# Decode attention plus FFN on one core: the sum is turned to five rows of 128 by a bf16 matmul, and the store has five runs of 256 B instead of 128 of 10 B

## Chip, cores and metric

The kernel runs on one core of one Trainium2 chip. The metric is device microseconds (us) of an execution, and quoted times are medians of a few runs. The *span* of a profile (first to last instruction) is about 1.6 us shorter than the time of the same run.

## The reference, cut to what matters

A decode step for one token: layer norm of `x` (640 numbers), attention of 32 heads over a cache of 32768 positions each, plus a SwiGLU FFN, plus the residual. The K and V caches are 537 MB and are read once.

```python
xn = _layernorm(x)
return x + _A_ref(xn, k_cache, v_cache, wq, wo) + _B_ref(xn, w_gate, w_up, w_down)
# _A_ref: q = xn @ wq; per head softmax(q k^T / sqrt(128)) v; then (32*128) @ wo -> 640
# _B_ref: (silu(xn @ w_gate) * (xn @ w_up)) @ w_down -> 640
```

## The kernel before

K and V of each head go whole (8.4 MB) through a ring of three slots, asked for by one queue (SP). VectorE (DVE) multiplies K by q, TensorE (PE) adds up the scores and multiplies P by V. After the last head comes the tail, which is all that this study is about. The last V is loaded in five pieces of 128, 64, 32, 16 and 16 column blocks, each with its semaphore.

```python
wd_v = wd.rearrange("p j (m c) -> p j m c", c=NCD)      # NCD = 5
wo_v = wo.rearrange("p h (m c) -> p h m c", c=NCD)
acc = ps8[:, 6, 0:NCD]                                  # PSUM, output m*5+c at [m, c]
...
def pv_last():                                          # PE
    for i, n in enumerate(TAIL):                        # 128, 64, 32, 16, 16
        t.wait_ge(s_tail[i], 16)
        for _ in range(n):
            mm = t.matmul(OL, lhsT=ring[:, s, j * DH:(j + 1) * DH], rhs=P[:, h % PR, j:j + 1], ...)   # L292
def att(h):
    for c in range(NCD):                                # weights 10 B apart
        mm = t.matmul(acc[:, c:c + 1], lhsT=wo_v[:, h, :, c], rhs=ocol[:, h:h + 1], ...)              # L358
...
fold(H - 2)
t.wait_ge(s_wo, 16)
t.wait_ge(s_ov, H)
for h in range(H - 1):
    att(h)                                              # 155 matmuls
total(H - 1)
pv_last()                                               # 256 matmuls
t.wait_ge(s_ov, H + 1)
att(H - 1).then_inc(s_att, 1)                           # 5 matmuls
...
v.wait_ge(s_att, 1)                                     # DVE
v.tensor_tensor(out=outb[:, :], in0=xf[:, :], in1=acc, op=ALU.add).then_inc(s_fin, 1)
...
e.wait_ge(s_fin, 1)                                     # SP: 128 runs of 10 B
e.dma_start(out[0, 0:1, :].rearrange("o (p c) -> (o p) c", c=NCD), outb[:, :]).then_inc(s_out, 16)
```

Of the kernel before, what the change touches and what calls it, by code (L numbers as in the profile page):

```python
# [5 lines left out]
ALU = mybir.AluOpType  # L6
ACTF = mybir.ActivationFunctionType
AX = mybir.AxisListType
BF16 = mybir.dt.bfloat16
F32 = mybir.dt.float32  # L10


def bass_parallel_sum__gqa_block_cached__swiglu_ffn__decode_kernel(
# [18 lines left out]
    NCD = D // 128  # L32
# [41 lines left out]
    with ExitStack() as es:  # L74
        def sbt(name, shape, dtype):
            return es.enter_context(nc.sbuf_tensor(name, shape, dtype))

        def sem(name):
            return es.enter_context(nc.semaphore(name))
# [5 lines left out]
        ident = sbt("ident", [128, 128], BF16)  # L85
# [3 lines left out]
        ocol = sbt("ocol", [128, H], BF16)  # L89
        hcol = sbt("hcol", [128, FB], BF16)  # L90
        sg = sbt("sg", [128, 2, FB], F32)
        one1 = sbt("one1", [1, 1], BF16)
        xf = sbt("xf", [128, NCD], F32)
        xc = sbt("xc", [128, NCD], F32)
        xq = sbt("xq", [128, NCD], F32)
        xn = sbt("xn", [128, NCD], BF16)
        outb = sbt("outb", [128, NCD], BF16)
# [8 lines left out]
        s_x, s_wq, s_wo, s_out = sem("x"), sem("wq"), sem("wo"), sem("o")  # L106
# [10 lines left out]
        s_fpd, s_fx = sem("ffn_down"), sem("ffn_x")  # L117
        s_exp, s_pv, s_o4, s_fold, s_ov = sem("exp"), sem("pv"), sem("o4"), sem("fold"), sem("ov")
        s_f, s_fa, s_fd = sem("ffn_pe"), sem("ffn_act"), sem("ffn_dve")
        s_att, s_fin = sem("att"), sem("fin")  # L120
        block = es.enter_context(nc.Block())

        flat = ring[:, :, :].rearrange("p s n -> p (s n)")
# [2 lines left out]
        xrow = flat[0:1, x0 + NCD * 128:x0 + NCD * 128 + D]  # L126
# [8 lines left out]
        wd = flat[:, d0:d0 + FB * D].rearrange("p (j d) -> p j d", j=FB)  # L135
        assert 2 * NCD * F + FB * D <= CE
        wg_v = wg.rearrange("p (c n) -> p c n", c=NCD)
        wu_v = wu.rearrange("p (c n) -> p c n", c=NCD)
        wd_v = wd.rearrange("p j (m c) -> p j m c", c=NCD)

        def hidden(w, c, j):
            if j < FM:
                return w[:, c, 0:FM * 128].rearrange("p (m j) -> p m j", j=FM)[:, :, j]
            return w[:, c, FM * 128:F]
        wo = flat[:, WO_S * CE:WO_S * CE + H * D].rearrange("p (h n) -> p h n", h=H)
        wo_v = wo.rearrange("p h (m c) -> p h m c", c=NCD)
        assert H * D <= CE

        def kv_src(cache, h, j0, n):
            return cache[0, h].rearrange("(p j) d -> p (j d)", p=128)[:, j0 * DH:(j0 + n) * DH]  # L150
# [20 lines left out]
        with nc.psum_tensor("ps8", [128, 8, 512], F32) as ps8:  # L171
# [3 lines left out]
            acc = ps8[:, 6, 0:NCD]  # L175
            fold_ps = ps8[:, 6, 8:9]
            misc = ps8[:, 7, :]

            @block.sync
            def sp(e):  # L180
                owner = {}
                for u in units:
                    s = slot_of[u]
                    if s in owner:
                        e.wait_ge(*owner.pop(s))
                    if u[0] == "wq":
                        e.dma_start(wq, A_wq.rearrange("(p c) n -> p (c n)", c=NCD)).then_inc(s_wq, 16)
                        owner[s] = (s_q, NQB)
                    elif u[0] == "k":
                        e.dma_start(ring[:, s, :], kv_src(A_k_cache, u[1], 0, NJ)).then_inc(s_slot[s], 16)  # L190
                        owner[s] = (s_qk, NHF * (u[1] + 1))
                    elif u == LASTV:
                        j = 0
                        for i, n in enumerate(TAIL):
                            e.dma_start(ring[:, s, j * DH:(j + n) * DH],
                                        kv_src(A_v_cache, u[1], j, n)).then_inc(s_tail[i], 16)
                            j += n
                    elif u[0] == "v":
                        e.dma_start(ring[:, s, :], kv_src(A_v_cache, u[1], 0, NJ)).then_inc(s_slot[s], 16)
                        owner[s] = (s_pv, u[1] + 1)  # L200
                    elif u[0] == "ffn":
                        e.dma_start(wg, B_w_gate.rearrange("(p c) n -> p (c n)", c=NCD)).then_inc(s_ffn, 16)
                        e.dma_start(wu, B_w_up.rearrange("(p c) n -> p (c n)", c=NCD)).then_inc(s_ffn, 16)
                        e.dma_start(flat[:, d0:d0 + FM * D], B_w_down[0:FM * 128, :].rearrange(  # L204
                            "(p j) n -> p (j n)", j=FM)).then_inc(s_ffn, 16)
                        e.dma_start(wd[0:FL, FM, :], B_w_down[FM * 128:F, :]).then_inc(s_ffn, 16)
                        owner[s] = (s_fpd, 1)
                    else:
                        e.dma_start(wo, A_wo.rearrange("(h d) n -> d h n", d=DH)).then_inc(s_wo, 16)
                e.wait_ge(s_fin, 1)  # L210
                e.dma_start(out[0, 0:1, :].rearrange("o (p c) -> (o p) c", c=NCD), outb[:, :]).then_inc(s_out, 16)
                e.wait_ge(s_out, 16)

            @block.gpsimd
# [8 lines left out]
            def pe(t):  # L223
# [2 lines left out]
                t.wait_ge(s_a, 2)  # L226
                for c in range(NCD):
                    mm = t.matmul(misc[:, 8 + c:9 + c], lhsT=xrow_v[:, :, c], rhs=one1[:, :], start=True, stop=True)
                mm.then_inc(s_pa, 1)

                t.wait_ge(s_a, 4)
# [6 lines left out]
                for b in range(NQB):  # L238
                    for c in range(NCD):
                        mm = t.matmul(bank[b], lhsT=xnb[:, c, :], rhs=wq_v[:, c, b * 512:(b + 1) * 512],  # L240
                                      start=(c == 0), stop=(c == NCD - 1))
# [97 lines left out]
                for off, w in ((0, wg_v), (FB, wu_v)):  # L339
                    for j in range(FB):  # L340
                        n = 128 if j < FM else FL
                        for c in range(NCD):
                            mm = t.matmul(misc[0:n, off + j:off + j + 1], lhsT=hidden(w, c, j),  # L343
                                          rhs=xn[:, c:c + 1], start=(c == 0), stop=(c == NCD - 1))
# [3 lines left out]
                for j in range(FB):  # L348
                    n = 128 if j < FM else FL
                    for c in range(NCD):  # L350
                        mm = t.matmul(acc[:, c:c + 1], lhsT=wd_v[0:n, j, :, c], rhs=hcol[0:n, j:j + 1],
                                      start=first, stop=(j == FB - 1), skip_group_check=True)
                        first = False
                mm.then_inc(s_fpd, 1)

                def att(h):
                    for c in range(NCD):
                        mm = t.matmul(acc[:, c:c + 1], lhsT=wo_v[:, h, :, c], rhs=ocol[:, h:h + 1],  # L358
                                      start=(h == 0 and c == 0), stop=(h == H - 1), skip_group_check=True)
                    return mm  # L360

# [11 lines left out]
                for h in range(H - 1):  # L373
                    att(h)
                total(H - 1)
                pv_last()
                t.wait_ge(s_ov, H + 1)
                att(H - 1).then_inc(s_att, 1)

            @block.scalar  # L380
            def act(a):
# [53 lines left out]
            def dve(v):  # L435
                n_a = [0]

                def step(ins):
                    ins.then_inc(s_a, 1)
                    n_a[0] += 1  # L440
                    v.wait_ge(s_a, n_a[0])
# [2 lines left out]
                step(v.memset(one1[:, :], 1.0))  # L444
                v.wait_ge(s_pa, 1)
                step(v.tensor_copy(out=xf[:, :], in_=misc[:, 8:8 + NCD]))
                step(v.tensor_reduce(out=st[:, 0:1], in_=xf[:, :], axis=AX.X, op=ALU.add))
                v.wait_ge(s_pa, 2)
                step(v.tensor_scalar(out=st[:, 1:2], in0=misc[:, 0:1], scalar1=1.0 / D, scalar2=None,
# [18 lines left out]
                n = 0  # L468
# [14 lines left out]
                    v.wait_ge(s_fd, n)  # L483

                v.wait_ge(s_fpd, 1)
                v.tensor_tensor(out=xf[:, :], in0=xf[:, :], in1=acc, op=ALU.add).then_inc(s_fx, 1)

                group, wait = counter(v, H0)

# [45 lines left out]
                h = H - 1  # L535
# [2 lines left out]
                v.tensor_scalar(out=ocol[:, h:h + 1], in0=OL, scalar1=rzb[:, h % SR:h % SR + 1],  # L538
                                scalar2=None, op0=ALU.mult).then_inc(s_ov, 1)
                v.wait_ge(s_att, 1)  # L540
                v.tensor_tensor(out=outb[:, :], in0=xf[:, :], in1=acc, op=ALU.add).then_inc(s_fin, 1)


# [26 lines left out]
```

## Time and profile before

| | before |
|---|---|
| median of 3 runs (range) | 1294.11 us (1293.77 to 1294.47) |
| span of the profiled run | 1292.1 us |
| read from HBM | 554 MB at 429 GB/s over the span |
| store: issue to full semaphore | 2.82 us |

The first view is the page of the kernel before. The rows are 40 equal slices of the span: busy tenths of the DMA engines, and what they moved.

```profile
span 1292.1 us, 9830 instructions
...
DMA  9999999999999999999999999999999999999997
GB/s 400 449 424 427 443 425 435 436 434 428 436 434 438 428 436 438 426 434 438 426 434 438 430 432 436 434 432 432 438 434 428 436 438 426 434 438 428 432 401 315
...
q1 hardware_dynamic: 14704, 554.00, 99.5%
q8 instruction: 9, 0.15, 0.0%
```

The DMA engines are the limit in all slices but the last. So a change that does not touch the loads can act only in the tail, some 20 us.

The second view is the end of the chain that ended last in the kernel before: start, length, what.

```profile
1277.65 0.43 PE ps L310 x2
1278.07 1.63 PE ps L292 x61
1279.70 0.23 issue
1279.93 3.55 PE ps L292 x128
1283.48 2.38 issue
1285.86 1.94 PE ps L292 x67
...
1287.82 0.23 DVE ocol L538
...
1288.10 0.37 PE ps L358 x5
...
1288.50 0.16 DVE outb L541
```

"issue" is time in which the engine waited for nothing that the profile knows of. There are two such gaps among the matmuls on the last V (L292), exactly 128 matmuls apart. The third view is the timeline around this stretch: the 155 projection matmuls ahead of it, and the sum and the store issue at its end.

```profile
1271.32 6.33 PE L358 MATMUL ps<-ocol,ring 128*128 128x1 bf16 x155 [0.36 <-ACT ocol L408]
...
1288.50 0.16 DVE L541 TENSOR_TENSOR outb<-xf,ps 128x5 bf16<-128x5 f32 x1 [0.45 <-PE ps L358]
1288.69 0.35 SPq L211 DMA_DIRECT2D out_dram<-outb  x1
```

The last view is what the queue's own engine waited for at the end (total, times, longest, in us).

```profile
SPq L74 <- DMA out_dram<-outb: 2.5, 1, 2.5
```

So a store of 1280 B holds the kernel for 0.35 us of issue and 2.5 us of waiting.

### The profile page before, as it was taken

The page shows a single profiled execution, that of the slowest core. Times are in us where ns is not written, and L with a number is a line of the kernel's source. Part 1 is how long each engine was busy: PE and PEld are TensorE (multiplying, and loading weights), DVE is VectorE, ACT ScalarE, POOL GpSimd, SP SyncE. Part 2 cuts the span into 40 slices and gives each one's busy share as a digit, 9 for nine tenths or more (in the row PEclk, how much of TensorE's full clock was granted, in tenths as well). Part 3 has the DMA queues.
Part 4 walks back from the last instruction along what each step waited for, and adds up shares of the span by engine and source line. Part 5 has one row for each costly group of instructions (what it writes and reads, how often), then busy time and mean ns, then how long its engine had stood idle before and what let it go on. Part 6 is the DMA issues. An engine that isn't in the chain of part 4 may idle for free.

```text
span 1292.1 us, 9830 instructions
## 1 busy us (share of the span) xinstructions
PE 1036.7 (80%) x5147; PEld 263.8 (20%) x3227; DVE 669.9 (52%) x407; ACT 51.9 (4%) x139; POOL 1.1 (0%) x8
## 2 busy tenths in 40 slices
PE   3678879877779877778877778877778877778977
PEld 1301222111222111222111222111222111222115
DVE  0485444666444666444666444666444666444560
ACT  2000000000000000000000000000000000000000
POOL 0000000000000000000000000000000000000000
PEclk9588899888889888899888899888889888889886
DMA  9999999999999999999999999999999999999997
GB/s 400 449 424 427 443 425 435 436 434 428 436 434 438 428 436 438 426 434 438 426 434 438 430 432 436 434 432 432 438 434 428 436 438 426 434 438 428 432 401 315
DMA packets 14717, 554.16 MB, mean 429 GB/s; under 512 B 1329, under 2 KB 5490, under 8 KB 5746
## 3 DMA queue, kind: packets, MB, share of 16 engines
q1 hardware_dynamic: 14704, 554.00, 99.5%
q8 instruction: 9, 0.15, 0.0%
q14 instruction: 2, 0.02, 0.0%
q10 hardware_dynamic: 2, 0.00, 0.0%
HBM read 553.99 MB, written 0.00 MB: 429 GB/s over the span
## 4 chain that ended last, share of the span: by engine, by line
DMA 52%; PE 29%; DVE 12%; issue 6%; SPq 0%; DVEq 0%; ACT 0%
DMA ring<-in_A_k_cache_dram 52%; PE ps L279 17%; DVE ring L504 12%; PE ps L248 9%; PE ps L267 1%; PE ps L292 1%; PE ps L358 1%; PE ps L316 0%; PE ps L310 0%; PE ps L302 0%; DVEq L504 0%; SPq L204 0%; DVE sc L510 0%; PE ps L322 0%; ACT o L403 0%
## 5 line engine op out<-in xcount | busy, mean ns | idle before, releaser
L504 DVE TENSOR_TENSOR ring<-ring,qb 128x8192 bf16<-128x8192 bf16 x128 | 557.8, 4420 | 86.6 <-DMA ring<-in_A_k_cache_dram 86.5
L248 PE MATMUL ps<-ring,ident 128*128 128x512 bf16 x1920 | 496.0, 417 | 0.0
L279 PE MATMUL ps<-ring,P 128*4 128x512 bf16 x1984 | 438.3, 379 | 0.0
L267 PE MATMUL ps<-ring,ident 128*128 128x512 bf16 x128 | 56.1, 438 | 224.2 <-DVE ring L504 223.7
L279 PEld LDWEIGHTS ps<-ring,P 128*4 128x4 bf16 x1984 | 166.0, 85 | 245.4
L267 PEld LDWEIGHTS ps<-ring,ident 128*128 128x128 bf16 x128 | 12.6, 98 | 620.4 <-DVE ring L504 326.4
L522 DVE TENSOR_SCALAR negb<-ps 128x1 f32<-128x1 f32 x32 | 5.1, 158 | 215.5 <-PE ps L322 215.5
L510 DVE TENSOR_REDUCE sc<-ps 128x64 f32<-128x512 f32 x128 | 82.3, 684 | 62.6 <-PE ps L248 62.6
L519 DVE TENSOR_REDUCE m<-ps 1x1 f32<-1x128 f32 x32 | 8.9, 279 | 192.2 <-PE ps L316 192.2
L412 ACT ACTIVATE P<-sc,negb 128x256 bf16<-128x256 f32 x32 | 16.2, 508 | 1179.6 <-DVE negb L522 1179.6
L302 PE MATMUL ps<-identf,o 4*128 4x1 f32 x248 | 31.9, 245 | 0.9 <-ACT o L403 0.9
L310 PEld LDWEIGHTS ps<-rsum,ones 128*128 128x128 f32 x64 | 12.3, 194 | 99.0 <-issue 98.2
L302 PEld LDWEIGHTS ps<-identf,o 4*128 4x128 f32 x248 | 30.0, 187 | 0.9 <-ACT o L403 0.9
L403 ACT ACTIVATE o<-ps,rzb 4x512 f32<-4x512 f32 x31 | 21.0, 677 | 0.0
L240 PE MATMUL ps<-ring 128*128 128x512 bf16 x40 | 10.2, 420 | 11.2 <-DMA ring<-in_A_wq_dram 11.2
L473 DVE TENSOR_SCALAR sg<-sg 128x13 f32<-128x13 f32 (+1 forms) x2 | 0.2, 156 | 34.3 <-ACT sg L393 34.3
L516 DVE TENSOR_REDUCE pmax<-sc 128x1 f32<-128x256 f32 x32 | 13.4, 420 | 0.0
L343 PE MATMUL ps<-xn,ring 128*128 128x1 bf16 (+1 forms) x140 | 8.7, 198 | 5.7 <-DMA ring<-in_B_w_down_dram 5.7
L316 PE MATMUL ps<-identf,pmax 128*1 128x128 f32 x64 | 12.2, 272 | 1.2 <-DVE pmax L516 1.2
L322 PE MATMUL ps<-m,ones 1*128 1x1 f32 x64 | 12.1, 256 | 0.4 <-DVE m L519 0.4
L322 PEld LDWEIGHTS ps<-m,ones 1*128 1x128 f32 x64 | 9.4, 182 | 14.2 <-issue 13.5
L492 DVE RECIPROCAL rzb<-ps 128x1 f32<-128x1 f32 x32 | 5.0, 158 | 9.8 <-PE ps L310 9.8
(50 smaller groups left out, 88.2 us busy)
## 6 DMA issues: line engine op xcount, KB each, us to landing
ring<-in_A_wq_dram SPq DMA_DIRECT2D x1, 5120.0 KB, 15.3
ring<-in_A_wo_dram SPq DMA_DIRECT2D x1, 5120.0 KB, 37.0
ring<-in_A_v_cache_dram SPq DMA_DIRECT2D x1, 4096.0 KB, 22.2
ring<-in_B_w_gate_dram SPq DMA_DIRECT2D x1, 2160.0 KB, 19.9
ring<-in_B_w_up_dram SPq DMA_DIRECT2D x1, 2160.0 KB, 24.6
ring<-in_B_w_down_dram SPq DMA_DIRECT2D x1, 2080.0 KB, 28.6
ring<-in_A_v_cache_dram SPq DMA_DIRECT2D x1, 2048.0 KB, 21.6
ring<-in_A_v_cache_dram SPq DMA_DIRECT2D x1, 1024.0 KB, 23.6
```

Of the source, the lines that this page charges most:

```text
L248: return t.add_instruction(mybir.InstMatmult(start_tensor_calc=False, stop_tensor_calc=stop, tile_size=(128, 128), tile_position=(0, 0), l ...
L267: t.matmul(ob, lhsT=ident[:, :], rhs=src, start=True, stop=False)
L279: mm = t.matmul(O, lhsT=P[:, h % PR, j:j + W], rhs=ring[:, s, j * DH:(j + W) * DH], start=(j == 0), stop=(j + W == NJ))
L292: mm = t.matmul(OL, lhsT=ring[:, s, j * DH:(j + 1) * DH], rhs=P[:, h % PR, j:j + 1], start=(j == 0), stop=(j == NJ - 1))
L302: mm = t.matmul(fold_ps, lhsT=o4[:, m * DH:(m + 1) * DH], rhs=identf[0:W, m:m + 1], start=(m == 0), stop=(m == W - 1))
L322: t.matmul(misc[:, 128:129], lhsT=ones[0:1, :], rhs=m1[0:1, h % SR:h % SR + 1], start=True, stop=True).then_inc(s_b, 1)
L358: mm = t.matmul(acc[:, c:c + 1], lhsT=wo_v[:, h, :, c], rhs=ocol[:, h:h + 1], start=(h == 0 and c == 0), stop=(h == H - 1), skip_group_che ...
L403: a.activation(out=o4[:, :], in_=O, func=ACTF.Copy, scale=rzb[0:W, h % SR:h % SR + 1]).then_inc(s_o4, 1)
L412: a.activation(out=P[:, h % PR, :], in_=sc[:, :], func=ACTF.Exp, bias=negb[:, h % SR:h % SR + 1], scale=c_scale, accum_out=rsum[:, h % SR: ...
L504: v.tensor_tensor(out=kh, in0=kh, in1=q[:, None, :].to_broadcast([128, HF, DH]), op=ALU.mult).then_inc(s_mul, 1)
L510: v.tensor_reduce(out=sc[:, i * HF:(i + 1) * HF], in_=bank[i].rearrange("p (j e) -> p j e", e=G), axis=AX.X, op=ALU.add).then_inc(s_red, 1)
L516: v.tensor_reduce(out=pmax[:, h % SR:h % SR + 1], in_=sc[:, :], axis=AX.X, op=ALU.max).then_inc(s_max, 1)
```

## The change

Its intent is a shorter store. The output is kept as [m, c] with output number `c*128+m`, so that five rows of 128 are whole runs of 256 B. One bf16 matmul with the identity turns the 128x5 sum to 5x128, DVE copies it out of PSUM, and the store has five runs. A second copy of x in that order (`xr`) is made at the start. The order of the columns also changes how the weights of `wo` and `w_down` are read: side by side instead of 10 B apart.

```diff
-        wd_v = wd.rearrange("p j (m c) -> p j m c", c=NCD)
+        wd_v = wd.rearrange("p j (c m) -> p j c m", c=NCD)
-        wo_v = wo.rearrange("p h (m c) -> p h m c", c=NCD)
+        wo_v = wo.rearrange("p h (c m) -> p h c m", c=NCD)
+            orow_ps = ps8[0:NCD, 5, 128:256]
...
-                e.wait_ge(s_fin, 1)
-                e.dma_start(out[0, 0:1, :].rearrange("o (p c) -> (o p) c", c=NCD), outb[:, :]).then_inc(s_out, 16)
+                e.wait_ge(s_fin, 2)
+                e.dma_start(out[0, 0:1, :].rearrange("o (c m) -> (o c) m", c=NCD), orow[:, :]).then_inc(s_out, 16)
...
+                for c in range(NCD):
+                    mm = t.matmul(misc[:, 16 + c:17 + c], lhsT=xrow[:, c * 128:(c + 1) * 128], rhs=one1[:, :],
+                                  start=True, stop=True)
...
-                        mm = t.matmul(acc[:, c:c + 1], lhsT=wo_v[:, h, :, c], rhs=ocol[:, h:h + 1],
+                        mm = t.matmul(acc[:, c:c + 1], lhsT=wo_v[:, h, c, :], rhs=ocol[:, h:h + 1],
...
                 att(H - 1).then_inc(s_att, 1)
+                t.wait_ge(s_fin, 1)
+                t.matmul(orow_ps, lhsT=outb[:, :], rhs=ident[:, :], start=True, stop=True).then_inc(s_or, 1)
...
-                v.tensor_tensor(out=outb[:, :], in0=xf[:, :], in1=acc, op=ALU.add).then_inc(s_fin, 1)
+                v.tensor_tensor(out=outb[:, :], in0=xr[:, :], in1=acc, op=ALU.add).then_inc(s_fin, 1)
+                v.wait_ge(s_or, 1)
+                v.tensor_copy(out=orow[:, :], in_=orow_ps).then_inc(s_fin, 1)
```

(The same edit on `wd_v`'s matmul, the semaphores, the buffers and the copy to `xr` are cut.)

More of the change, by code (lines that the diff above doesn't have):

```diff
@@ L93, in bass_parallel_sum__gqa_block_cached__swiglu_ffn__decode_kernel @@
         xf = sbt("xf", [128, NCD], F32)
+        xr = sbt("xr", [128, NCD], F32)
+        orow = sbt("orow", [NCD, 128], BF16)
         xc = sbt("xc", [128, NCD], F32)
@@ L120, in bass_parallel_sum__gqa_block_cached__swiglu_ffn__decode_kernel @@
         s_att, s_fin = sem("att"), sem("fin")
+        s_xr, s_or = sem("xr"), sem("orow")
         block = es.enter_context(nc.Block())
@@ L350, in pe @@
                     for c in range(NCD):
-                        mm = t.matmul(acc[:, c:c + 1], lhsT=wd_v[0:n, j, :, c], rhs=hcol[0:n, j:j + 1],
+                        mm = t.matmul(acc[:, c:c + 1], lhsT=wd_v[0:n, j, c, :], rhs=hcol[0:n, j:j + 1],
                                       start=first, stop=(j == FB - 1), skip_group_check=True)
@@ L446, in dve @@
                 step(v.tensor_copy(out=xf[:, :], in_=misc[:, 8:8 + NCD]))
+                v.tensor_copy(out=xr[:, :], in_=misc[:, 16:16 + NCD]).then_inc(s_xr, 1)
                 step(v.tensor_reduce(out=st[:, 0:1], in_=xf[:, :], axis=AX.X, op=ALU.add))
@@ L485, in dve @@
                 v.wait_ge(s_fpd, 1)
-                v.tensor_tensor(out=xf[:, :], in0=xf[:, :], in1=acc, op=ALU.add).then_inc(s_fx, 1)
+                v.wait_ge(s_xr, 1)
+                v.tensor_tensor(out=xr[:, :], in0=xr[:, :], in1=acc, op=ALU.add).then_inc(s_fx, 1)
                 group, wait = counter(v, H0)
```

## The prediction

> **What bounds the kernel now.** The page says DMA: 554 MB at 429 GB/s, DMA row 9 in all slices but the last. The median is 1294.11 us, the span 1292.1. All but a tail of some 20 us is reading K and V, which the change does not touch. So only the tail can move the time.
>
> **The tail before** (timeline of the last 40 us, chain of waits):
> - 1271.32 to 1277.65: 155 output-projection matmuls (L358), 41 ns apart.
> - 1277.9 to 1287.8: 256 matmuls on the last V (L292), 27.5 ns apart while they run, with two idle gaps called "issue": 0.23 us at 1279.7 and 2.38 us at 1283.48, exactly 128 matmuls apart.
> - By the trace's semaphore updates the last five V pieces landed at 1275.9, 1280.8, 1283.3, 1284.5 and 1285.7. The matmul that ended the long gap waits for no semaphore, and 16 KB packets on the instruction queue start at 1277.4, 1283.5 and 1287.0. So I read the gap as instruction fetch, not data. The Trainium skill ("Runtime: NRT & Kernel Launch", Instruction fetch mechanics) says that instructions come in 16 KiB blocks of 256; 128 weight loads and 128 matmuls are that number, which agrees.
> - 1287.82 ocol, 1288.10 five matmuls, 1288.50 sum (163 ns), 1288.69 store issue (348 ns); the semaphore is full at 1291.51; end 1292.1.
>
> **What the change does.**
> 1. *Adds* in the last chain: a hop to PE (0.04 us, as from ocol to L358), one matmul (198 ns for the first L358, plus 127 more columns at the granted clock 0.5, about 106 ns), a hop, and a copy of 5x128 (158 ns for one column at L522, plus about 130 ns for 128, estimated from the 128x256 reduce of 420 ns). Together +0.65 us (0.5 to 0.8), fully on the path.
> 2. *Removes* most of the store's spread. From issue end to last landing it takes 2.47 us: first packet after 0.49 us, 144 packets within 0.2 us, then the 16 engines' semaphore updates from 1289.94 to 1291.51. The first engine is back 0.41 us after the first packet, the last 1.8 us. I take that spread as writes of 10 B into shared lines of HBM. Five whole 256 B runs should behave like the first engine: -1.3 us (estimate, -0.2 to -1.6). [...]
> 3. *Unstated in the title:* `wo` and `w_down` weights are now read with columns side by side instead of 10 B apart. L358 should go from 41 ns to L292's 27.5, so the 155 end 2.1 us earlier; L351 saves 1.1 us at 42 us, hidden under the DMA. The 2.1 us let PE reach each instruction block sooner, so the fetch is asked for sooner; the floor is the last V piece (1285.74 + 16 matmuls + drain, 1286.4 against 1287.8). Estimate -0.7 us (0 to -1.4).
> 4. Five more matmuls and a copy at 2.1 us: hidden, as the weights of L240 land at 16.1.
>
> **Sum:** 0.65 - 1.3 - 0.7 = -1.35 us: 1292.8 us, 1291.6 to 1294.2. Far inside 2%.
>
> **What would show it.** L358 mean spacing near 27 ns; the long L292 gap shorter or earlier; between sum and store issue +0.65 us; store issue to landing near 1.3 us instead of 2.8; everything before 1270 us unmoved.
>
> **What would make it wrong.** A fixed write receipt (then about 1294); block boundaries falling worse, with the gap kept; a slow PE wake-up or copy; DMA noise of a few tenths (runs before: 1293.77 to 1294.47).

## The result, and the profile after

After takes 1292.66 us (median of 4, 1291.66 to 1292.86) against 1293.94 us for before in the same rounds. The ratio is 0.9988, with a 95% interval of 0.9971 to 1.0006: the same within 2%, and the interval is not clear of zero, though the runs themselves do not overlap (the slowest of after, 1292.86, lies under the fastest of before, 1293.46). A ratio here is the mean time of one kernel's runs over that of the other's of the same rounds, so it is not quite the ratio of the medians. Executions over 1.5% slower than the fastest of the same kernel are left out of the means. A second measurement (after_again, 5 runs) gave 1292.59 against 1293.84, again without overlap. I had expected 1.2 us below before, and gaps that end near 1279.6 and 1285.8; the time fell by 1.25 us, and the gaps ended at 1280.00 and 1286.21.

The page after:

```profile
span 1291.1 us, 9843 instructions
...
DMA  9999999999999999999999999999999999999998
...
q1 hardware_dynamic: 14570, 554.00, 99.6%
q8 instruction: 9, 0.15, 0.0%
```

The end of the chain after:

```profile
1275.59 0.43 PE ps L317 x2
1276.01 0.07 issue
1276.08 1.63 PE ps L299 x56
1277.71 1.86 issue
1279.58 3.55 PE ps L299 x128
1283.13 2.66 issue
1285.79 2.08 PE ps L299 x72
...
1287.88 0.23 DVE ocol L549
...
1288.16 0.31 PE ps L365 x5
...
1288.49 0.17 DVE outb L552
...
1288.71 0.28 PE ps L387
...
1289.01 0.28 DVE orow L554
```

The timeline of the projection and of the store issue after, and what SP waited for:

```profile
1271.43 4.15 PE L365 MATMUL ps<-ocol,ring 128*128 128x1 bf16 x155 [0.35 <-ACT ocol L417]
...
1289.32 0.36 SPq L215 DMA_DIRECT2D out_dram<-orow  x1
```

```profile
SPq L74 <- DMA out_dram<-orow: 0.8, 1, 0.8
```

| Stage (us) | before | after | change |
|---|---|---|---|
| 155 projection matmuls | 6.33 | 4.15 | -2.18 |
| start of the sum | 1288.50 | 1288.49 | 0.0 |
| start of the sum to store issue | 0.19 | 0.83 | +0.64 |
| store issue to full semaphore | 2.82 | 1.19 | -1.63 |
| span | 1292.1 | 1291.1 | -1.0 |

The last two changes make up the span's change: 0.64 - 1.63 = -0.99. The odd line is the first: PE saved 2.2 us in the projection and then started the sum at the same moment. The gap at 1277.71 grew from 0.23 to 1.86 us. The experiments ask where that went, and why the old store was so slow.

### The profile page after: what moved, and what is told of

It reads as the page before. It is cut to its first block, busy times and chain, and to the rows that moved or that the text cites. A ratio compares the mean times of both kernels' runs of the same rounds, so it can differ in the third digit from the quotient of the medians.

```text
span 1291.1 us, 9843 instructions
## 1 busy us (share of the span) xinstructions
PE 1039.1 (80%) x5152; PEld 261.2 (20%) x3233; DVE 670.2 (52%) x409; ACT 51.9 (4%) x139; POOL 1.1 (0%) x8
## 4 chain that ended last, share of the span: by engine, by line
DMA 52%; PE 31%; DVE 11%; issue 6%; SPq 0%; DVEq 0%; ACT 0%
DMA ring<-in_A_k_cache_dram 52%; PE ps L286 17%; PE ps L255 11%; DVE ring L515 11%; PE ps L274 1%; PE ps L299 1%; PE ps L365 0%; PE ps L323 0%; PE ps L317 0%; PE ps L309 0%; DVEq L515 0%; SPq L208 0%; DVE sc L521 0%; PE ps L329 0%; ACT o L412 0%
## 5 line engine op out<-in xcount | busy, mean ns | idle before, releaser
L299 PE MATMUL ps<-P,ring 128*128 128x1 bf16 x256 | 7.2, 165 | 4.6 <-issue 4.5
```

## The experiments

Two questions. **A: what is the gap in the last-V matmuls?** *Fetch theory*: PE waits for its next 16 KB block of instructions (128 weight loads and 128 matmuls). *Data theory*: it waits for the last V piece, which lands at 1285.74 in before and 1285.96 in after. **B: what made the old store slow?** The number of runs, their size, a fixed receipt, or something that the runs share.

Eleven runs of ten kernels follow, after_again among them. "V landed" is the last semaphore update of the last V piece in the trace's records, and packets are those of the instruction queue (q8), from the same records.

### layout_only (wrong result)

```diff
-wd_v = wd.rearrange("p j (m c) -> p j m c", c=NCD)     # before, weights alone changed; wo_v and the
+wd_v = wd.rearrange("p j (c m) -> p j c m", c=NCD)     # two matmuls likewise
```

> Before with only the wo and w_down reads changed to columns side by side (result wrong on purpose: columns permuted). Fetch theory (the long gap in the last-V matmuls is instruction fetch, asked for when the sequencer dispatches the block ahead, not when the array gets there): the 155 projection matmuls take 4.1 to 4.2 us instead of 6.3, the gap stays and ends within 0.3 us of 1285.86, time within 0.3 us of before. My prediction's theory (the 2.1 us reach the fetch): gap ends 0.7 us or more earlier and the time falls by about 0.7 us. Data theory (the gap waits for the last V piece): gap ends when that piece lands, at 1285.7 to 1286.0, time unchanged.

Measured: 1293.61 us against 1293.86 (5 and 9 runs), ratio 0.9996, interval 0.9983 to 1.001. The timeline:

```profile
1271.96 4.19 PE L358 MATMUL ps<-ocol,ring 128*128 128x1 bf16 x155 [0.35 <-ACT ocol L408]
...
1280.30 3.55 PE L292 MATMUL ps<-P,ring 128*128 128x1 bf16 x128 [1.85 <-issue]
...
1286.23 1.93 PE L292 MATMUL ps<-P,ring 128*128 128x1 bf16 x67 [2.37 <-issue]
```

The projection fell to 4.19 us, and the first gap grew to 1.85 us: the same exchange as in after, with no turn and no new store. The gap's end, 1286.23, misses the 0.3 us that I had allowed (0.37 off), but this run's tail is late as a whole: its V landed at 1286.40, 0.66 us after before's. The gap ended 0.17 us before V landed, so it did not wait for the last piece, and the pieces that the next 35 matmuls need had landed by 1283.93. The interval, -2.2 to +1.3 us, holds zero and the predicted -0.7 us alike, so the times alone do not decide. The trace says more: the last-V matmuls ended 1.76 us after V landed, against 2.05 us in before, so at most some 0.3 us was gained here and not 0.7. The clock is no rival for the faster projection: the clock of before fell from 1.0 to 0.5 at 1271.7 us and that of after at 1273.3 us, but the matmuls of before are 40 ns apart on both sides of the fall, and those of after 25 and then 27 ns.

### store_only (wrong result)

```diff
-e.dma_start(out[0, 0:1, :].rearrange("o (p c) -> (o p) c", c=NCD), outb[:, :])
+e.dma_start(out[0, 0:1, :].rearrange("o (c m) -> (o c) m", c=NCD), orow[:, :])   # orow: zeros, set at the start
```

> Before, but the store is five runs of 256 B from a tile of zeros made at the start (result wrong on purpose). If the store's gain and the turn's cost simply add: issue to landing 1.2 us instead of 2.8, sum to issue unchanged at 0.19 us, time 1.6 us below before. If the gain in after came from elsewhere (the tail before the store): within 0.5 us of before.

Measured: 1292.23 us against 1293.86, so -1.63 us; ratio 0.9988 (0.9974 to 1.0001). The semaphore is full 1.18 us after issue, and the sum stays 0.19 us ahead of it. SP waited for it as in after:

```profile
SPq L74 <- DMA out_dram<-orow: 0.8, 1, 0.8
```

The interval just reaches 1, but no run of store_only (1292.16 to 1292.40) comes near one of before (1293.44 to 1294.52). The size of the store's part, 1.63 us, is the same in the time and in the trace.

### turn_only (wrong result)

```diff
-e.dma_start(out[0, 0:1, :].rearrange("o (c m) -> (o c) m", c=NCD), orow[:, :])   # after
+e.dma_start(out[0, 0:1, :].rearrange("o (p c) -> (o p) c", c=NCD), outb[:, :])
```

> After, but after the turn the store is that of before: 128 runs of 10 B from the sum tile (result wrong on purpose: permuted). Expect sum start to store issue 0.83 us as in after, issue to landing 2.8 us as in before, time 0.65 us above before (0.4 to 0.9). A rival, that the shorter store in after is only an earlier wake-up or luck of that run, would give issue to landing near 1.2 us here too.

Measured: 1294.13 us against 1293.86, ratio 1.0002 (0.9988 to 1.0015). Sum to issue is 0.83 us and issue to full semaphore 2.74 us, both as expected, and SP waits as in before:

```profile
SPq L74 <- DMA out_dram<-outb: 2.4, 1, 2.4
```

The time rose by 0.27 us only, under my 0.4 to 0.9. I had left out that this kernel also has the new layout. The medians of the three kernels add up: layout and turn +0.27, store -1.63, together -1.36, against -1.25 to -1.28 for after. They would put the layout at 0.27 - 0.64 = -0.37 us, and layout_only puts it at -0.25; none of these is clear of the noise.

### shift24

The theories of the gap differ in what ties it down. 24 more pairs of weight load and matmul at the start of the program move every later instruction by 48 places; there, under the first loads, they should cost nothing.

```diff
+                for _ in range(24):          # after, at the start of PE's program
+                    mm = t.matmul(misc[:, 20:21], lhsT=xrow[:, 512:640], rhs=one1[:, :], start=True, stop=True)
                 mm.then_inc(s_pa, 1)
```

> After, with 24 more pairs of weight load and 1-column matmul at the start of the program (hidden under the first loads). Fetch theory: every 16 KB boundary moves 24 pairs earlier in the program, so the two gaps come after 32 and 160 of the last V's matmuls instead of 56 and 184, still 128 apart; first packet up to 0.6 us earlier, gap ends near 1279.0 and 1285.2, end of the last-V matmuls within 0.4 us of after's 1287.85. Data theory, or any wait tied to a given instruction: the gaps stay after 56 and 184.

Measured (one look, state unknown): 1292.13 us.

```profile
1275.93 0.99 PE L301 MATMUL ps<-P,ring 128*128 128x1 bf16 x32
1278.41 3.68 PE L301 MATMUL ps<-P,ring 128*128 128x1 bf16 x128 [1.49 <-issue]
...
1284.62 2.70 PE L301 MATMUL ps<-P,ring 128*128 128x1 bf16 x96 [2.53 <-issue]
```

The gaps come after 32 and 160 matmuls instead of 56 and 184. The matmuls after which PE used to stop now run through. No wait on a semaphore and no piece of data moves with the place in the program; a block of instructions does. The data theory falls here. The kernels above show the same without having been meant to: after has five more pairs at the start than before, and its first gap comes after 56 matmuls instead of 61, while layout_only, which has no more pairs than before, keeps 61. The miss: the gaps ended 1.2 us earlier, not 0.6, and the last-V matmuls ended 0.53 us earlier, beyond my 0.4.

### light_tail (wrong)

```diff
-e.dma_start(ring[:, s, j * DH:(j + n) * DH], kv_src(A_v_cache, u[1], j, n)).then_inc(s_tail[i], 16)   # after
+e.dma_start(ring[:, s, j * DH:j * DH + DH], kv_src(A_v_cache, u[1], j, 1)).then_inc(s_tail[i], 16)
```

> After, but each piece of the last V loads one column block only (0.16 MB instead of 8.4 MB; result wrong on purpose), so the DMA engines are idle from about 1266 us. Fetch theory with latency made by the full DMA queues: from resuming to the next block ready 3.5 us or less instead of 6.2, so both gaps fall under 0.5 us and the 256 matmuls take about 7.5 us in all instead of 11.7. If the fetch latency does not depend on the data traffic: gaps of 1.9 and 2.7 us stay, although no data is waited for. Data theory: no gaps at all, which the fetch theory tells apart only by small gaps still 128 matmuls apart.

Measured (one look): 1287.93 us. The data is wrong by design; the comparison with the reference cannot see the last head's stale V.

```profile
1275.81 7.09 PEld L299 LDWEIGHTS ps<-P,ring 128*128 128x128 bf16 x256
1276.02 6.96 PE L299 MATMUL ps<-P,ring 128*128 128x1 bf16 x256
```

256 matmuls in one piece, no gap. The records of the instruction queue say why. "Passed to packet" is from PE's first matmul past a 16 KB boundary to the start of the next 16 KB packet; "packet to resume" is from that packet to the matmul that ends the gap.

| second block (us) | passed to packet | packet to resume | gap |
|---|---|---|---|
| before | 3.61 | 2.33 | 2.38 |
| after | 3.62 | 2.59 | 2.66 |
| after_again | 3.65 | 2.55 | 2.66 |
| layout_only | 3.35 | 2.57 | 2.37 |
| store_only | 3.02 | 2.37 | 1.84 |
| turn_only | 3.72 | 2.49 | 2.66 |
| shift24 | 3.66 | 2.55 | 2.53 |
| att_early (below) | 3.71 | 2.49 | 1.28 |
| light_tail | 0.46 | at most 2.96 (no wait) | 0 |

With the DMA engines busy, a block takes about 6 us from request to use, while its 128 pairs take 3.55 us to run. With the engines idle the packet starts after 0.46 us and nothing waits (one look, but a difference of over 2.5 us to every other row). So what the PE gains inside a block it waits for at the next boundary. That the request is made when PE passes into the block before is an inference: it fits all rows, and 0.46 us with idle DMA engines leaves little room for anything else. There is a rival: in before, after, after_again and shift24 the packet starts within 0.11 us of the moment when PE runs out of instructions, so those rows would also fit a request made only then. Other rows exclude it: the packet starts 0.53 us before that moment in store_only, 1.21 us before it in att_early, and 3.1 us before it in light_tail.

### att_early, and att_early_again

If the request is the limit, the work that leads to it must start sooner. The projection of heads 0 to 29 needs only the fold of head 29. The last fold goes to another PSUM bank, to keep it apart from the sums that are being built up.

```diff
-                fold(H - 2)                      # after
                 t.wait_ge(s_wo, 16)
-                t.wait_ge(s_ov, H)
-                for h in range(H - 1):
+                t.wait_ge(s_ov, H - 1)
+                for h in range(H - 2):
                     att(h)
+                fold(H - 2)                      # into fold_last = ps8[:, 0, 0:1]
+                t.wait_ge(s_ov, H)
+                att(H - 2)
```

> After, but the projection of heads 0 to 29 starts when the fold of head 29 is out, about 2.1 us sooner, and the fold of head 30 comes after it (in another PSUM bank). Fetch theory: the block requests come about 2 us sooner (packets near 1275.1 and 1281.2), the two gaps end near 1277.5 and 1283.7, the end is then set by the last V piece at 1285.96 plus 16 matmuls and drain, last matmul near 1286.4 to 1286.7; time 1.0 to 1.3 us below after, 2.0 to 2.6 below before. Data theory: the long gap still ends at 1285.7 to 1286.0 and the time equals after (1.0 to 1.3 below before).

> The early projection once more beside after on one chip: 1.1 us below after (0.8 to 1.4), 2.3 below before; last-V matmuls end within 0.7 us of the last V piece's landing.

Measured: 1291.56 us against 1293.86 (ratio 0.9982, 0.9968 to 0.9996), and 1291.40 against 1293.84, where after took 1292.59: 1.19 us below after, 2.4 below before. The five runs (1291.33 to 1291.64) lie under all five of after (1292.20 to 1293.09). Both results are correct.

```profile
1269.61 4.00 PE L366 MATMUL ps<-ocol,ring 128*128 128x1 bf16 x150 [0.35 <-ACT ocol L420]
...
1281.06 1.66 PE L300 MATMUL ps<-P,ring 128*128 128x1 bf16 x56 [1.21 <-DMA ring<-in_A_v_cache_dram]
1283.99 1.63 PE L300 MATMUL ps<-P,ring 128*128 128x1 bf16 x56 [1.28 <-issue]
...
1286.03 0.59 PE L300 MATMUL ps<-P,ring 128*128 128x1 bf16 x16 [0.40 <-DMA ring<-in_A_v_cache_dram]
```

The packets start at 1275.34 and 1281.50 instead of 1277.14 and 1283.20 in after. The gap ends at 1283.99, and the last waits are now for the data: the last V piece landed at 1285.98, and the matmuls ended 0.63 us later, instead of 1.88 us in after. This is the best version here.

### att_early_before

The same edit on the kernel before.

> Before (10 B apart weights, 128 runs of 10 B) with the early projection alone. Fetch theory: the requests come earlier here too, so the end of the last-V matmuls comes within 1.0 us of the last V piece's landing instead of 1.9, and the time is 0.8 to 1.4 us below before, about what early projection gains on after. If the faster projection is needed for it: less than 0.4 us below before.

Measured: 1293.46 us against 1293.84, ratio 0.9998 (0.9984 to 1.0011). The result is correct. This is a miss for my fetch theory as I had stated it: 0.38 us gained, not 0.8 to 1.4, and the matmuls end 1.47 us after V landed.

```profile
1278.45 5.18 PE L293 MATMUL ps<-P,ring 128*128 128x1 bf16 x189
...
1285.48 1.92 PE L293 MATMUL ps<-P,ring 128*128 128x1 bf16 x67 [1.85 <-issue]
```

Here the first gap is gone (189 in one piece), because PE itself is late. At 41 ns a matmul the projection of heads 0 to 29 takes 6.13 us, the last-V matmuls start at 1278.45 instead of 1276.25 in att_early, and PE passes the boundary at 1280.08 instead of 1277.79. The next packet then starts at 1282.89 instead of 1281.50. So the fast weights and the early start do not add: alone they gave 0.25 us (layout_only) and 0.38 us, neither clear of the noise. Together they gave what is left of att_early's 2.3 to 2.4 us after the turn and the store (0.99 us): about 1.3 to 1.45 us.

### store_shapes and store_shapes2

Question B, by itself: after the sum, 12 and then 13 shapes of store to scratch in HBM, three rounds, each waited for before the next. The real store comes last, so the results are correct.

```diff
+                for _ in range(3):                       # after, on SP
+                    for dst, src in probes:              # scratch[:, 0:n] of [rows, pitch] <- rows x n of an SBUF tile
+                        e.dma_start(dst, src).then_inc(s_out, 16)
+                        n_out += 16
+                        e.wait_ge(s_out, n_out)
```

> After, with 12 shapes of store to scratch in HBM ahead of the real one, each waited for before the next, three rounds of all (result right, time longer by some 60 us). Issue to landing, us. Shared-line theory (10 B writes by different engines into the same stretch of HBM are done one after the other): 128x10 B packed 2.8; the same at pitch 32 B and 64 B in between; at pitch 256 B and 512 B near 1.2 to 1.5; 64x20, 32x40 and 16x80 packed fall step by step from 2.8; 5x256 and 1x1280 near 1.2. Run-count theory (each small write costs its engine time, 8 per engine): 128x10 B is 2.8 at every pitch, 128x256 B packed also at least 2.8, and 16x10 B packed near 1.2. Fixed-receipt theory: all within 0.3 us of each other, which the after run already speaks against (1.19 against 2.82).

> After, with 13 more shapes of store to scratch ahead of the real one (result right). The first shape run showed 128x10 B packed at 2.5 to 3.1 us and the same runs at pitch 32 B or more at 1.4 us, 64x20 B packed at 1.6 us, so neither the number of runs nor their size is it; what neighbours share is. Word theory (two runs that share a 4 B word are slow): 10 B packed and 6 B packed and 2 B packed slow (2.3 us or more), 10 B at pitch 12 B, 12 B packed, 8 B packed, 10 B at pitch 16 and 20 B all near 1.4 to 1.7. Stretch theory (three or more runs inside the same 32 B are slow, whatever their alignment): 10 B at pitch 12 B, 12 B packed, 8 B packed slow too, 10 B at pitch 16 and 20 B fast. Alternating engines (neighbouring runs written by different engines at about the same time, from HBM): if the slow part is one engine writing the same place twice in a row, the far order is about 1 us faster than the near order from HBM; if it is the sharing itself, both are slow. Two interleaved halves of 64x10 B at pitch 20 B issued one after the other: under 2.2 us from the first issue if sharing between two separate transfers is harmless, 2.5 or more if not. Fewer runs packed (64, 32): slow by less, or not at all as for 16.

Issue to full semaphore, from the trace's records, three rounds each (one execution per kernel, idle DMA engines, the same order of shapes in each round):

| runs x bytes, pitch | us |
|---|---|
| 128 x 2, packed | 17.19, 17.31, 17.11 |
| 128 x 6, packed | 4.41, 4.77, 4.44 |
| 128 x 8, packed | 2.83, 2.85, 3.42 |
| 128 x 10, packed (the store before) | 2.76, 2.51, 3.14; second kernel 2.50, 3.27, 2.97 |
| 128 x 10, pitch 12 | 3.23, 2.17, 2.11 |
| 128 x 12, packed | 2.11, 3.15, 1.98 |
| 128 x 10, pitch 16 | 1.39, 2.19, 1.39 |
| 128 x 10, pitch 32, 64 | 1.41, 1.41, 1.47; 1.58, 1.42, 1.41 |
| 128 x 10, pitch 256, 512 | 1.39, 1.39, 1.39; 1.40, 1.39, 1.40 |
| 64 x 10 and 32 x 10, packed | 2.61, 2.48, 2.81; 2.45, 2.33, 2.14 |
| 16 x 10, packed | 1.29, 1.29, 1.29 |
| 64 x 10, pitch 20 | 1.64, 1.64, 1.65 |
| 64 x 20; 32 x 40; 16 x 80, packed | 1.66, 1.63, 1.64; 1.33, 1.33, 1.32; 1.30, 1.31, 1.31 |
| 128 x 256, packed | 1.46, 1.45, 1.45 |
| 5 x 256 (the store after) | 1.16, 1.14, 1.13 |
| 1 x 1280 | 1.07, 1.07, 1.08 |
| 128 x 10 packed from HBM, neighbours meant for one engine / for different engines (the kept trace does not tell the engine) | 3.04, 3.11, 3.35 / 2.76, 2.75, 2.94 |
| two interleaved halves of 64 x 10, from the first issue | 2.88, 2.76, 2.77 |

The waits of SP in the second kernel (total, times, longest) show the same order:

```profile
SPq L234 <- DMA scr_128x2B_at_2B<-P: 33.8, 2, 17.0
...
SPq L234 <- DMA scr_128x6B_at_6B<-P: 8.5, 2, 4.4
SPq L234 <- DMA scr_128x10B_at_10B<-P: 7.8, 3, 2.9
SPq L234 <- DMA scr_128x10B_at_12B<-P: 6.5, 3, 2.9
...
SPq L234 <- DMA scr_128x10B_at_16B<-P: 2.9, 2, 1.9
SPq L234 <- DMA scr_64x10B_at_20B<-P: 2.4, 2, 1.2
```

Not the number of runs: 128 of 256 B take 1.45 us. Not their size: 128 of 10 B take 1.39 us when they lie 256 B apart. Not a fixed receipt: the range is 1.07 to 17.3 us, so a part that is the same for all shapes can be 1.07 us at most. What counts is how close many runs begin to each other: 16 B or more is fast with one exception in three at 16 B, 12 B or less is slow, and 2 B is slowest by far. A pitch of 20 B is as fast with runs of 10 B as with runs of 20 B (1.64 us both), so it is not the gap between the runs either.

My word theory (a shared 4 B word) falls: 8 B and 12 B packed, which share no word, are slow. The stretch theory holds in kind, with its step between 12 and 16 B. It does not hold for 16 runs of 10 B, which are fast (16 packets of data; I take it that each went to an engine of its own). My step-by-step fall to 64x20, 32x40 and 16x80 did not come either: 64x20 is already fast (its first packet comes 0.3 us later than the others', which is the rest). The order meant to give neighbours to different engines helped by 0.35 us, the difference of the medians, not by 1, so, if the runs were dealt out as meant, one engine writing the same place twice is not the main part. What in the memory or in the engines does it is not settled. Two interleaved halves are no way around it, so the turn is worth its 0.64 us.

## Why the prediction was right or wrong

The time was right: 1292.8 predicted, 1292.66 and 1292.59 measured, inside 1291.6 to 1294.2. That range also holds before's own 1293.94, so the time alone proves little; the terms have to be looked at. Two terms of the sum were mis-sized, in opposite directions.

1. **The turn, +0.65 us**: right. 0.83 - 0.19 = 0.64 us in after, 0.83 us again in turn_only. (Its 106 ns for 127 columns can be worked out from the trace: at a granted clock of 1.0, L248 takes 3.24 us for 15 matmuls of 512 columns, 0.42 ns a column; twice that at 0.5.)
2. **The store, -1.3 us (-0.2 to -1.6)**: right in mechanism, too small. It measured -1.63 us, in the trace and in the time of store_only. I wrote that five whole runs should behave like the first engine. They did (0.41 us from the first packet to the last landing, the same 0.41), and the first packet also came 0.07 us sooner after issue. The low end of my range, -0.2, came from a misread page. The Trainium skill ("DMA: Bandwidth & Descriptors", Anatomy of one DMA) puts most of about 2 us on a write receipt for DMAs that GpSimd issues; this store is issued by SP, and that section says nothing of it. The store probes rule a fixed receipt of that size out here: stores of 1280 B or less took between 1.07 and 17.3 us. "Shared lines" was the right direction and not proved; the step lies between 12 and 16 B of pitch.
3. **The faster weights, -0.7 us**: this step failed. Its premises were right: 155 matmuls went from 41 to 27 ns apart, and the gap is instruction fetch (shift24). The step that failed is "The 2.1 us let PE reach each instruction block sooner, so the fetch is asked for sooner". Counting 256 PE instructions back from the first gap, the boundary before it lies inside the projection, and PE passes it at 1273.58 us in after and 1274.91 in before (an estimate from the order of the records): 1.33 us sooner, not 2.1. Of that, only 0.26 us arrived at the first packet, which started 3.56 us after this point instead of 2.50. From there on a block takes about 6 us from request to use while the DMA engines are full. The gap at the first boundary grew from 0.23 to 1.86 us and took back nearly all. The matmuls ended 2.05 and 2.02 us after V landed in before and store_only, and 1.88, 2.36, 1.85 and 1.76 us in after, after_again, turn_only and layout_only: no difference beyond the scatter. A part of the predicted gain may be there in the medians (0.25 to 0.37 us, inside my range of 0 to 1.4), which the intervals do not separate from zero. Why the first packet came so much later after that boundary is open. It is not one run's luck: the same count gives 2.5 to 2.9 us in the three kernels with weights 10 B apart and 3.2 to 3.7 us in the others under full load. A request made when the sequencer hands the instructions out, ahead of PE, would be one reason; no run tests it. In att_early, the same count has PE past that boundary 1.60 us sooner than in after, and the packet came 1.80 us sooner.
4. **Hidden work at the start**: right. The projection starts at 1271.43 against 1271.32, so nothing ahead of the tail moved beyond the scatter of the loads.
5. **The sum**: 0.64 - 1.63 = -0.99 us by the traces, -1.25 to -1.28 us by the medians. My -1.35 came from -0.33 us too little for the store and 0.3 to 0.7 us too much for the fetch. That the total was so close is luck.

The skill's account of fetching ("Runtime: NRT & Kernel Launch", Instruction fetch mechanics: blocks of 16 KiB, the next one fetched while the present one runs) agrees with the gaps 128 pairs apart. Its remark that the cost is "mostly hidden" does not hold in this tail, with gaps of up to 2.66 us.

## What to carry to other kernels

Look at the pitch of the runs of a small store, not only at their number: 128 runs that began 10 B apart cost this kernel 1.6 us more than five whole ones, and in the probes 128 runs of 2 B took 17 us. In this kernel's stretch of many short PE instructions under full DMA load, gaps called "issue" at every 256th instruction were instruction blocks on their way. Making the instructions faster mainly widened the gap; starting them earlier as well gained 1.2 us more, and starting slow ones earlier about 0.4 us, not clear of the noise. To see whether a gap belongs to data or to the place in the program, shift the program by a few cheap instructions and look whether the gap moves.

## What the Trainium skill lacked or had wrong

- "DMA: Bandwidth & Descriptors", Anatomy of one DMA: the breakdown of a fixed part of about 2 us is for DMAs that GpSimd issues, and the page has none for a store issued by SP. For such stores the runs show 1.07 us (1 x 1280 B) to 17.3 us (128 x 2 B packed) from issue to full semaphore, and 1.13 to 1.19 us for 5 x 256 B.
- "DMA: Bandwidth & Descriptors", Specifications: below 512 B the engine does read-modify-write. The page does not say that the pitch of small runs matters: 128 x 10 B cost 2.5 to 3.3 us packed and 1.39 us at a pitch of 256 B, no more than 128 x 256 B (1.45 us).
- "Runtime: NRT & Kernel Launch", Instruction fetch mechanics: the page calls the cost of a 16 KiB boundary mostly hidden. Under full DMA load the packet started 3.0 to 3.7 us after PE passed the boundary before, where PE had waited there, and PE went on 2.3 to 2.6 us later still; idle, the packet started after 0.46 us. The page gives no time for it.
- "TensorE: Matmul & The Clock Gate", Weight-path perf modes: it allows fast weight loads at column steps up to 1,024 elements and gives no time that a wider step costs. Pairs of load and 1-column matmul were 40 ns apart with columns 10 B apart, at a granted clock of 1.0 and of 0.5 alike (before; att_early_before), and with columns side by side 25 ns apart at 1.0 and 27 ns at 0.5 (after; layout_only).
